# Scores of a unit summed in one PSUM bank among the value products of the unit before it, w_o's last block in two loads, and one load for x

## The chip, the cores and the metric

The kernel runs on one NeuronCore of one Trainium2 chip. The metric is device time in microseconds: 217.72 us, the median of three runs (217.52 to 218.88). One further execution was taken by the hardware profiler; all rows shown come from it. The engines are PE (TensorE, matrix products), DVE (VectorE), ACT (ScalarE), POOL (GpSimd) and SP (SyncE), which only issues transfers here. Sixteen DMA engines move the data.

## The reference, cut to what matters

One decode step for two rows of x, all in float32: windowed attention over a cache, times a gate from a small gated MLP.

```python
# A_x (2,1,512); k_cache, v_cache (2,8,32768,128); wq (512,4096); wo (4096,512)
# w_in (512,1792); w_out (896,512)
W = 4096                                    # last 4096 keys of 32768
q = (xn @ wq)                               # 32 heads of 128; 4 query heads per kv head
scores = einsum("bhqd,bhkd->bhqk", q, k[last W]) * 128 ** -0.5
o = einsum("bhqk,bhkd->bhqd", softmax(scores), v[last W])
s = o.reshape(2, 1, 4096) @ wo
z = gelu(xn @ w_in); z1, z2 = halves of z
g = silu((z1 * (w_sp * layernorm(z2) + b_sp)) @ w_out)
out = x + s * g                             # xn = layernorm(x)
```

## The kernel before, in words

**Units.** A unit is one pair of kv heads of one batch row: 2 x 8 / 2 = 8 units, `units[0]` to `units[7]`, four per batch row. Each has 4 MB of K and 4 MB of V. A partition holds 64 consecutive keys of one of the two heads, so a K or V load is one transfer of 128 rows of 32 KB. The 64 keys are handled in four chunks of 16 (`m` = 0 to 3).

**The ring.** All large inputs go through one buffer of four slots of 4 MB. `enqueue` puts a load in a queue; `advance(slot)` marks a slot as free and issues the loads at the head of the queue whose slots are free. The order never changes: w_q (slots 0 and 1), w_in (2), w_out (3), then k0, k1, v0, k2, v1, k3, v2, and so on to k7, v6, v7, then w_o in pieces of 16, 8, 4, 1, 1, 1 and 1 blocks of (128 rows x 512). Slots are taken round robin, so v0 replaces w_in in slot 2, v1 replaces k0 in slot 0, k3 replaces k1, v2 replaces v0, k4 replaces k2, and so on. SP issues in this order, and a load in a slot waits until everything that reads the slot's former content is done: for K the four DVE transposes, for V the sixteen value products on PE. The result-shaped copy of x (`x4`, two loads, one per batch row) is issued behind the 16-block piece.

**One unit.** `turn(u, m)` transposes a chunk of K on DVE in 32 x 32 blocks into a tile `kt` (three buffers). `shares(u, m)` multiplies the query, for each quarter `dq` of the 128 features, into its own 32 partitions of a PSUM bank `sh`; ACT copies the bank to SBUF (`shs`), and `add_shares(u, m)` adds the four quarters with a 128 x 128 matrix `add_dq` of zeros and ones into the score bank `s`, where chunk m has its own rows. So a unit has sixteen score products, four copies and four adding products. In the profile every float32 product is two PE instructions. `share_max` takes the maximum from `s` on DVE with one small product on PE in between, `probs` the exponentials on ACT, and `probs_t` transposes them on DVE (`pT`). `values` forms sixteen products of V with `pT` into a bank `acc`, product j in the column group j % 4. `scale_out` copies `acc` (four ACT copies), and `collect` adds it into a bank for the batch row.

**Order.** `pe`, `dve`, `act` and `sp` are wrappers that keep each engine's instructions in the order in which the program gives them. In the loop over units (its rows in the profile all have the wrapper's line, L37) unit u and the one before it, `prev`, alternate: first transpose and shares of u; maximum and exponentials of prev; second transpose and shares of u; transposed probabilities and all sixteen value products of prev; then the third and fourth chunk of u; then `scale_out`, the release of u's K slot and of prev's V slot, and `collect`. So V of unit n - 1 comes free in iteration n. The last unit's value products, the sum over units and the products with w_o follow after the loop.

**Gate.** Ahead of the loop the MLP ends with a product `y` into four row groups; `spread_quarters` adds these with eight PE instructions of 128 columns into a bank of 128 x 128, from which DVE and ACT compute the gate. DVE's first K transpose follows the gate in DVE's order.

**End.** Blocks 0 to 27 of w_o are multiplied into `part`, copied and spread into `so`; blocks 28 to 31 go into `so` directly. Two DVE operations form the result, and SP stores it.

Of the kernel before, what the change touches and what calls it, by code (L numbers as in the profile page):

```python
# [9 lines left out]
F32 = mybir.dt.float32  # L10
AF = mybir.ActivationFunctionType
# [3 lines left out]
P = 128  # L15
HQ, DH = 32, 128
G = 4
# [25 lines left out]
def kernel(  # L43
# [13 lines left out]
    nc = tc.nc  # L57
# [9 lines left out]
    DC = D // G  # L67
# [36 lines left out]
    def bank(name, tag):  # L104
        return ps.tile([P, 512], F32, tag=tag, name=name, bufs=BANKS[tag])
# [15 lines left out]
    def by_group(t):  # L121

        return bass.AP(tensor=t.tensor, offset=t.offset, ap=[[DC, G], [D, B], [1, DC]])
# [16 lines left out]
    units = []  # L140
    for n in range(NU):
        u = Unit()
        u.n, u.kt, u.shs, u.slot = n, {}, {}, {}
# [37 lines left out]
    nc.gpsimd.memset(hT, 0.0)  # L181
    x4 = const("x4", DC)
    nc.gpsimd.memset(x4, 0.0)
    add_dq = const("add_dq", NCH - 1 + P)
    nc.gpsimd.memset(add_dq, 0.0)
    sel = const("sel", 56)
# [63 lines left out]
    nc.gpsimd.tensor_copy(sel4[:, 3 : 3 + 32 : 4], rowr)  # L250
    nc.gpsimd.tensor_mul(perm, ap(rowm, 0, [[1, 32], [0, G]]), ap(grpm, 0, [[0, 32], [1, G]]))
    perm = perm.rearrange("p h e -> p (h e)")
    for a in range(2):
# [40 lines left out]
    def q_of(u, dq):  # L294
        return ap(qbd, (u.n * 4 + dq) * 32, [[1, 32]])
# [74 lines left out]

    def turn(u, m):

        u.kt[m] = sb.tile([P, JC, DH], F32, tag="kt", name=f"kt{u.n}_{m}", bufs=3)
        dve.transpose(
            u.kt[m].rearrange("p j d -> p (j d)"), u.k[:, JC * m : JC * m + JC, :].rearrange("p j d -> p (j d)")
        )

    def shares(u, m):

        u.sh = bank(f"sh{u.n}_{m}", "sh")  # L380
        for dq in range(4):
            pe.matmul(
                u.sh[32 * dq : 32 * dq + 32, :], q_of(u, dq), u.kt[m][:, :, 32 * dq : 32 * dq + 32],
                start=True, stop=True,
            )
        u.shs[m] = sb.tile([P, 512], F32, tag="shs", name=f"shs{u.n}_{m}")
        act.activation(u.shs[m], u.sh, AF.Copy)

    def add_shares(u, m):

        if m == 0:
            u.s = bank(f"s{u.n}", "s")
        pe.matmul(u.s, add_dq[:, NCH - 1 - m : NCH - 1 - m + P], u.shs[m], start=(m == 0), stop=(m == NCH - 1))

    def share_max(u):
        m2 = sb.tile([P, 2], F32, tag="m2", name=f"m2_{u.n}")
# [28 lines left out]
    def weigh(u):  # L425
# [10 lines left out]
    def values(u, part=0, parts=1):  # L436
        if part == 0:
            u.acc = bank(f"acc{u.n}", "acc")
        n = JC // parts
        for j in range(n * part, n * part + n):  # L440
            c = j % G
            pe.matmul(
                u.acc[32 * c : 32 * c + 32, :], u.pT[:, j, :], u.v[:, j : J : JC, :],
                start=(j < G), stop=(j >= JC - G),
            )
# [12 lines left out]
    def collect(u, end=NU // B - 1):  # L458

        if u.n == 0:  # L460
            col[0] = bank("col", "col")
        r = slice(32 * u.b, 32 * u.b + 32)
        pe.matmul(
            col[0][r, :], sel[:, 24 - 8 * u.w : 56 - 8 * u.w], u.o.rearrange("p j d -> p (j d)"),
            start=(u.w == 0), stop=(u.w == end),
        )
# [24 lines left out]
    prev = old = None  # L491
    last = units[-1]
    for u in units:
        turn(u, 0)
        shares(u, 0)
        if old is not None and old.n == NU // B - 1:
# [24 lines left out]
    values(old, 0, 2)  # L521
    share_max(last)
    probs(last)
    values(old, 1, 2)
    advance(old.slot["v"])
    probs_t(last)
    weigh(last)
    scale_out(old)
    values(last, 0, 2)
    collect(old, old.w)  # L530
    early = slice(0, 32 * last.w)
    values(last, 1, 2)
    t = gather(last.b)
    scale_out(last)
    divide(last.b, t[early, :], early)
# [53 lines left out]
```

## Time and profile before

| | before |
|---|---|
| time, median of 3 runs | 217.72 us |
| the profiled execution's span | 215.6 us |
| PE busy | 144.9 us (67%) |
| DVE busy | 107.1 us (50%) |
| ACT busy | 43.7 us (20%) |
| bytes read from HBM | 89.40 MB, 415 GB/s over the span |
| granted PE clock, mean | 0.885 |

The span goes from the first to the last instruction of the profiled execution; the runs' times include some 2 us around it. In a timeline row stand the start and the duration in us, the engine, the operation, the tiles out<-in, partitions x elements and the count; in brackets the idle time before it and what ended that. SPq rows are issues of transfers by SP. In a row of the windowed view stand the stretch, its length, the busy time of PE, PE's weight loads, DVE, ACT and POOL with counts, the granted PE clock, the busy share of the DMA engines and GB/s. The line that starts with DMA gives the busy share of the DMA engines in tenths for 40 equal slices.

### The profile page before, as it was taken

The numbers are of one execution on the slowest core, as the hardware profiler recorded it, in microseconds if no ns is written. First come the engines' busy times: TensorE is split into PE (matmuls) and PEld (weight loads), VectorE is DVE, ScalarE is ACT, GpSimd is POOL, SyncE is SP. The second block draws the span as 40 slices with busy tenths as digits, with TensorE's granted clock in tenths as the row PEclk, the third lists the DMA queues.
The fourth block names the chain that finished last, engine by engine and source line by source line (L and its number), as shares of the span: only waits on it lengthen the run. The fifth ranks groups of instructions, "written<-read, shape, count | busy, mean of one in ns | idle before, by whom it ended". The sixth has DMA issues, their size and how long they took to land.

```text
span 215.6 us, 2181 instructions
## 1 busy us (share of the span) xinstructions
PE 144.9 (67%) x848; PEld 40.3 (19%) x848; DVE 107.1 (50%) x161; ACT 43.7 (20%) x108; POOL 4.2 (2%) x22
## 2 busy tenths in 40 slices
PE   0010787224595897699599499459949967987663
PEld 0010222100021222122122132112202211222311
DVE  1140025633995943953936663793585089233101
ACT  2030000331124115114303304130331231241001
POOL 6010000000000000000000000000000000000000
PEclk9999999658599699699799789859975996999998
DMA  9898999999999999999999999999999999999990
GB/s 389 390 389 389 431 423 459 435 438 421 450 395 474 395 453 419 444 432 425 439 404 450 419 444 429 432 432 419 444 413 447 425 432 444 425 435 404 410 376 33
DMA packets 3788, 89.52 MB, mean 415 GB/s; under 512 B 434, under 2 KB 450, under 8 KB 964
## 3 DMA queue, kind: packets, MB, share of 16 engines
q1 hardware_dynamic: 3772, 89.40, 96.9%
q8 instruction: 6, 0.10, 0.2%
q14 instruction: 2, 0.02, 0.0%
q10 hardware_dynamic: 8, 0.00, 0.0%
HBM read 89.40 MB, written 0.00 MB: 415 GB/s over the span
## 4 chain that ended last, share of the span: by engine, by line
DMA 41%; PE 39%; DVE 16%; ACT 2%; issue 2%; DVEq 0%
DMA ring<-in_A_wo_dram 20%; PE sh L37 11%; DMA ring<-in_A_k_cache_dram 11%; DVE kt L37 10%; DMA ring<-in_A_wq_dram 10%; PE s L37 10%; PE acc L37 7%; PE q_ps L37 4%; PE y L37 2%; PE z L37 1%; PE col L37 1%; PE mo L37 1%; DVE gate L37 1%; DVE u L37 1%; DVE qm L37 1%
## 5 line engine op out<-in xcount | busy, mean ns | idle before, releaser
L37 DVE STREAM_TRANSPOSE kt<-ring 128x2048 f32<-128x2048 f32 x32 | 72.2, 2286 | 24.9 <-DMA ring<-in_A_k_cache_dram 24.9
L37 PE MATMUL sh<-kt,qbd 128*32 128x512 f32 x256 | 43.6, 725 | 27.0 <-DVE kt L37 27.0
L37 ACT ACTIVATE shs<-sh 128x512 f32<-128x512 f32 x32 | 19.1, 597 | 99.4 <-PE sh L37 99.4
L37 PE MATMUL s<-shs,add_dq 128*128 128x512 f32 x64 | 39.0, 716 | 0.0
L37 PE MATMUL acc<-ring,pT 128*32 128x512 f32 x256 | 31.3, 614 | 0.0
L37 PEld LDWEIGHTS s<-shs,add_dq 128*128 128x128 f32 x64 | 11.0, 215 | 30.9 <-issue 26.5
L37 PEld LDWEIGHTS sh<-kt,qbd 128*32 128x32 f32 x256 | 7.0, 117 | 46.3 <-issue 38.3
L37 PE MATMUL q_ps<-ring,xnT 128*32 128x512 f32 x64 | 8.8, 713 | 7.6 <-DMA ring<-in_A_wq_dram 7.6
L37 PEld LDWEIGHTS acc<-ring,pT 128*32 128x32 f32 x256 | 7.8, 112 | 22.3 <-issue 17.6
L37 DVE TENSOR_REDUCE m<-s 128x2 f32<-128x512 f32 x8 | 5.4, 680 | 13.0 <-PE s L37 12.9
L37 PE MATMUL xnT_ps<-ident,xn 2*128 2x2 f32 x4 | 0.6, 252 | 14.5 <-DVE xn L37 14.5
L37 ACT ACTIVATE o<-acc,diag 128x128 f32<-128x128 f32 x30 | 8.6, 374 | 4.9 <-PE acc L37 4.9
L37 PE MATMUL part<-ring,oT 128*32 128x512 f32 x56 | 6.6, 597 | 3.5 <-DMA ring<-in_A_wo_dram 3.5
L37 ACT ACTIVATE p<-s,nb 128x256 f32<-128x256 f32 x16 | 7.6, 488 | 6.6 <-DVE nb L37 6.4
L37 DVE STREAM_TRANSPOSE qT<-q_ps 128x512 f32<-128x512 f32 x2 | 1.4, 717 | 14.4 <-PE q_ps L37 14.3
L37 PE MATMUL col<-o,sel 128*32 128x512 f32 x14 | 7.3, 601 | 0.0
L37 DVE TENSOR_TENSOR res<-so,gate 128x128 f32<-128x128 f32 x1 | 0.3, 292 | 11.5 <-PE so L37 11.5
L37 DVE STREAM_TRANSPOSE pT<-p 128x512 f32<-128x512 f32 x8 | 5.4, 674 | 1.2 <-ACT p L37 1.2
L37 PE MATMUL y<-ring,hT 128*32 128x512 f32 x14 | 3.3, 996 | 3.8 <-DVE hT L37 3.8
L37 ACT ACTIVATE zs<-z 128x448 f32<-128x448 f32 x1 | 0.5, 544 | 24.7 <-PE z L37 24.7
L37 ACT ACT_TABLE_LOAD x4 | 5.1, 1283 | 0.8 <-PEq L575 0.7
L37 PEld LDWEIGHTS q_ps<-ring,xnT 128*32 128x32 f32 x64 | 2.5, 130 | 13.1 <-issue 13.1
(114 smaller groups left out, 62.2 us busy)
## 6 DMA issues: line engine op xcount, KB each, us to landing
ring<-in_A_k_cache_dram SPq DMA_DIRECT2D x8, 4096.0 KB, 20.0
ring<-in_A_v_cache_dram SPq DMA_DIRECT2D x8, 4096.0 KB, 28.1
ring<-in_A_wo_dram SPq DMA_DIRECT2D x1, 4096.0 KB, 33.2
ring<-in_B_w_in_dram SPq DMA_DIRECT2D x1, 3584.0 KB, 17.1
ring<-in_A_wo_dram SPq DMA_DIRECT2D x1, 2048.0 KB
ring<-in_B_w_out_dram SPq DMA_DIRECT2D x1, 1792.0 KB, 21.0
ring<-in_A_wo_dram SPq DMA_DIRECT2D x1, 1024.0 KB
ring<-in_A_wo_dram SPq DMA_DIRECT2D x4, 256.0 KB, 17.6
```

What stands on the lines that cost most here:

```text
L37: return self.tc.keep_in_program_order(call(*args, **kwargs))
```

## The change

Scores: the products of a chunk m now go into the row group m of one bank and are summed there over the four quarters (`scores`, two chunks per call). A unit has one copy and one product with a new 128 x 128 matrix `regroup` (`by_key_group`) in place of four copies and four adding products. Between the score products of two chunks, which use two of PE's four column groups, stand eight value products of an older unit in the other two column groups: with chunks 0 and 1 the second half of unit u - 2, with chunks 2 and 3 the first half of unit u - 1. So the V of unit u - 2 is closed, and its slot given back, in iteration u (`close`). `kt` has four buffers. The last unit uses `shares` and `add_shares` for its last two chunks, and its end is written out anew. The gate's `y` is formed by one product over 512 columns and four ACT copies. w_o's last block is loaded as rows 0 to 99 and rows 100 to 127, and x4 in one load.

```diff
+    rows = [slice(0, P)], [slice(0, 100), slice(100, P)]
...
-                sp.dma_start(t[:, a : a + n, :], wo_v[:, j : j + n, :])
+                for r in rows[j == 31]:
+                    sp.dma_start(t[r, a : a + n, :], wo_v[r, j : j + n, :])
...
-                for b in range(B):
-                    sp.dma_start(x4[16 * b : P : 32, :], x[b].rearrange("o (g c) -> (o g) c", g=G))
+                sp.dma_start(x4[0:P:16, :], by_group(x))
...
+    for a in range(2):
+        nc.gpsimd.tensor_copy(regroup[:, :, a], ap(ident, 16 * a, [[4, G], [1, REP], [32, NCH]]))
...
-    y = bank("yq", "mo")[:, :DC]
-    spread_quarters(y, ys)
+    yp = bank("yq", "mo")
+    pe.matmul(yp, same, ys, start=True, stop=True)
+    y = const("y", DC)
+    for g in range(G):
+        r = slice(32 * g, 32 * g + 32)
+        act.activation(y[r, :], yp[r, g * DC : (g + 1) * DC], AF.Copy)
...
-        u.kt[m] = sb.tile([P, JC, DH], F32, tag="kt", name=f"kt{u.n}_{m}", bufs=3)
+        u.kt[m] = sb.tile([P, JC, DH], F32, tag="kt", name=f"kt{u.n}_{m}", bufs=4)
...
+    def columns(c):
+        return [j for j in range(JC) if j % G in c]
+
+    def scores(u, ms, v=None):
+        if ms[0] == 0:
+            u.sh = bank(f"sh{u.n}", "sh")
+        js = columns([c for c in range(G) if c not in ms]) if v is not None else []
+        for dq in range(4):
+            for m in ms:
+                pe.matmul(
+                    u.sh[32 * m : 32 * m + 32, :], q_of(u, dq), u.kt[m][:, :, 32 * dq : 32 * dq + 32],
+                    start=(dq == 0), stop=(dq == 3),
+                )
+            for j in js[2 * dq : 2 * dq + 2]:
+                value(v, j)
+
+    def by_key_group(u, rows=P, stop=True):
+        sh = sb.tile([P, 512], F32, tag="shs", name=f"shs{u.n}")
+        act.activation(sh[:rows, :], u.sh[:rows, :], AF.Copy)
+        u.s = bank(f"s{u.n}", "s")
+        pe.matmul(u.s, regroup[:rows, :], sh[:rows, :], start=True, stop=stop)
...
+    def close(u):
+        scale_out(u)
+        advance(u.slot["v"])
+
     for u in units:
+        prev = units[u.n - 1] if u.n > 0 else None
+        old = units[u.n - 2] if u.n > 1 else None
         turn(u, 0)
-        shares(u, 0)
...
         if prev is not None:
             share_max(prev)
             probs(prev)
         turn(u, 1)
-        shares(u, 1)
-        add_shares(u, 0)
+        scores(u, (0, 1), old)
+        if old is not None:
+            close(old)
         if prev is not None:
             probs_t(prev)
             weigh(prev)
-            if u is not last:
-                values(prev)
-        for m in range(2, NCH):
-            turn(u, m)
-            shares(u, m)
-            add_shares(u, m - 1)
-        if u is not last and prev is not None:
-            scale_out(prev)
+        if u is last:
+            break
+        turn(u, 2)
+        turn(u, 3)
+        scores(u, (2, 3), prev)
         advance(u.slot["k"])
-        add_shares(u, NCH - 1)
-        if u is not last and prev is not None:
-            advance(prev.slot["v"])
-            collect(prev)
-        old, prev = prev, u
...
+        by_key_group(u)
+        if old is not None:
+            collect(old)
```

Behind the loop the last unit's third and fourth chunk follow with `shares`, then the sixteen value products of the unit before it, in three groups around the maximum of the last unit's scores, and then the last unit's value products as before.

More of the change, by code (lines that the diff above doesn't have):

```diff
@@ L142 @@
         u = Unit()
-        u.n, u.kt, u.shs, u.slot = n, {}, {}, {}
+        u.n, u.kt, u.shs, u.slot, u.acc = n, {}, {}, {}, None
         u.b, u.w = divmod(n, NU // B)
@@ L183 @@
     nc.gpsimd.memset(x4, 0.0)
+    regroup = const("regroup", G, 2, REP, NCH)
     add_dq = const("add_dq", NCH - 1 + P)
@@ L252 @@
     perm = perm.rearrange("p h e -> p (h e)")
+    for a in range(2):
+        nc.gpsimd.tensor_copy(regroup[:, :, a], ap(ident, 16 * a, [[4, G], [1, REP], [32, NCH]]))
+    regroup = regroup.rearrange("p g a h m -> p (g a h m)")
     for a in range(2):
@@ L376, in turn, with value @@
         )
+    def value(u, j):
+        if u.acc is None:
+            u.acc = bank(f"acc{u.n}", "acc")
+        c = j % G
+        pe.matmul(
+            u.acc[32 * c : 32 * c + 32, :], u.pT[:, j, :], u.v[:, j : J : JC, :],
+            start=(j < G), stop=(j >= JC - G),
+        )
[7 more added lines that the diff above has]
+            for m in ms:
+                pe.matmul(
+                    u.sh[32 * m : 32 * m + 32, :], q_of(u, dq), u.kt[m][:, :, 32 * dq : 32 * dq + 32],
+                    start=(dq == 0), stop=(dq == 3),
+                )
+            for j in js[2 * dq : 2 * dq + 2]:
[5 more added lines that the diff above has]
+        pe.matmul(u.s, regroup[:rows, :], sh[:rows, :], start=True, stop=stop)
     def shares(u, m):
-        u.sh = bank(f"sh{u.n}_{m}", "sh")
+        t = bank(f"sh{u.n}_{m}", "sh")
         for dq in range(4):
             pe.matmul(
-                u.sh[32 * dq : 32 * dq + 32, :], q_of(u, dq), u.kt[m][:, :, 32 * dq : 32 * dq + 32],
+                t[32 * dq : 32 * dq + 32, :], q_of(u, dq), u.kt[m][:, :, 32 * dq : 32 * dq + 32],
                 start=True, stop=True,
@@ L386, in shares @@
         u.shs[m] = sb.tile([P, 512], F32, tag="shs", name=f"shs{u.n}_{m}")
-        act.activation(u.shs[m], u.sh, AF.Copy)
+        act.activation(u.shs[m], t, AF.Copy)
     def add_shares(u, m):
-        if m == 0:
-            u.s = bank(f"s{u.n}", "s")
-        pe.matmul(u.s, add_dq[:, NCH - 1 - m : NCH - 1 - m + P], u.shs[m], start=(m == 0), stop=(m == NCH - 1))
+        pe.matmul(u.s, add_dq[:, NCH - 1 - m : NCH - 1 - m + P], u.shs[m], start=False, stop=(m == NCH - 1))
     def share_max(u):
@@ L434, in weigh @@
         dve.reciprocal(wd[:, u.b : u.b + 1], u.mo[:, 32:33])
[L436 to L445, printed above, removed]
     def scale_out(u):
@@ L489, in collect_last @@
         divide(u.b, ol[r, :], r)
-    prev = old = None
+    def close(u):
+        scale_out(u)
+        advance(u.slot["v"])
     last = units[-1]
     for u in units:
+        prev = units[u.n - 1] if u.n > 0 else None
+        old = units[u.n - 2] if u.n > 1 else None
         turn(u, 0)
-        shares(u, 0)
-        if old is not None and old.n == NU // B - 1:
+        if u.n == NU // B + 2:
             divide(0, gather(0))
@@ L506 @@
             weigh(prev)
-            if u is not last:
-                values(prev)
-        for m in range(2, NCH):
-            turn(u, m)
-            shares(u, m)
-            add_shares(u, m - 1)
-        if u is not last and prev is not None:
-            scale_out(prev)
-        advance(u.slot["k"])
-        add_shares(u, NCH - 1)
-        if u is not last and prev is not None:
-            advance(prev.slot["v"])
-            collect(prev)
-        old, prev = prev, u
-    values(old, 0, 2)
+        if u is last:
[3 more added lines that the diff above has]
+        scores(u, (2, 3), prev)
+        advance(u.slot["k"])
+        by_key_group(u)
+        if old is not None:
+            collect(old)
+    turn(last, 2)
+    shares(last, 2)
+    by_key_group(last, 64, stop=False)
+    collect(old)
+    turn(last, 3)
+    add_shares(last, 2)
+    shares(last, 3)
+    advance(last.slot["k"])
+    first, second = columns((0, 1)), columns((2, 3))
+    both = [j for p in zip(first[::2], first[1::2], second[::2], second[1::2]) for j in p]
+    for j in both[:4]:
+        value(prev, j)
+    add_shares(last, 3)
+    for j in both[4:10]:
+        value(prev, j)
     share_max(last)
     probs(last)
-    values(old, 1, 2)
-    advance(old.slot["v"])
+    for j in both[10:]:
+        value(prev, j)
     probs_t(last)
     weigh(last)
-    scale_out(old)
-    values(last, 0, 2)
-    collect(old, old.w)
+    close(prev)
+    for j in range(8):
+        value(last, j)
+    collect(prev, prev.w)
     early = slice(0, 32 * last.w)
-    values(last, 1, 2)
+    for j in range(8, JC):
+        value(last, j)
     t = gather(last.b)
```

## The prediction

> **What bounds the kernel now.** I read the page's head, the busy slices and the DMA queues first, then the windowed view with bytes per stretch, then the DMA issues in order of time.
>
> ```profile
> span 215.6 us, 2181 instructions
> PE 144.9 (67%) x848; PEld 40.3 (19%) x848; DVE 107.1 (50%) x161; ACT 43.7 (20%) x108; POOL 4.2 (2%) x22
> DMA  9898999999999999999999999999999999999990
> q1 hardware_dynamic: 3772, 89.40, 96.9%
> q8 instruction: 6, 0.10, 0.2%
> 0.00:92.00 92.00, 47.96 (x274) 13.49 (x278) 44.72 (x83) 16.89 (x35) 4.19 (x22) 0.87 0.99 423
> 0.00:208.00 208.00, 141.24 (x796) 39.22 (x800) 106.50 (x159) 43.14 (x107) 4.19 (x22) 0.89 0.99 426
> ```
>
> No compute engine is busy for more than 67%, while the sixteen DMA engines are busy in every slice up to the last, on one queue of 89.40 MB (in the window rows the last two numbers are the DMA share and GB/s). Between 92 and 208 us it moved 0.426 x 208 - 0.423 x 92 = 49.7 MB in 116 us: 428 GB/s without a hole. So matrix, copy and transpose work counts only where it delays a transfer, or after the last byte. Nothing in the change alters the bytes.
>
> The end of the stream, by half microseconds and then two rows of the timeline:
>
> ```profile
> 209.50:210.00 0.50, 0.50 (x8) 0.06 (x8) 0.00 (x0) 0.00 (x0) 0.00 (x0) 1.00 0.71 262
> 210.00:210.50 0.50, 0.50 (x16) 0.26 (x8) 0.00 (x0) 0.00 (x0) 0.00 (x0) 1.00 0.53 201
> 210.50:211.00 0.50, 0.49 (x16) 0.16 (x8) 0.00 (x0) 0.40 (x1) 0.00 (x0) 1.00 0.42 160
> 211.00:211.50 0.50, 0.38 (x17) 0.25 (x13) 0.00 (x0) 0.20 (x1) 0.00 (x0) 1.00 0.26 98
> ...
> 209.41 1.07 PE L37 MATMUL part<-ring,oT 128*32 128x512 f32 x8 [0.58 <-DMA ring<-in_A_wo_dram]
> 213.12 0.60 SPq L37 DMA_DIRECT2D out_dram<-res  x1
> ```
>
> The engines do not finish together: the share falls in steps from 209.5 to 211.5. Spread evenly, those bytes would end at 209.5 + 0.5 x (0.71 + 0.53 + 0.42 + 0.26) = 210.46, so the slowest engines are 1.0 us behind the mean. At 210.5 to 211 a share of 0.42 is six or seven of sixteen engines, and six 16 KB instruction packets ran on the same engines (q8 above): I take each to have made one engine late. With some 100 of 1,696 PE instructions gone there will still be six. The last products follow, and the result leaves at 213.12. The execution's span is 215.6; the median of the runs, 217.72, is 2.1 us more, and I carry that over unchanged.
>
> **The part that decides: when a V slot comes free.** The ring has four 4 MB slots, filled in the order k0, k1, v0, k2, v1, k3, v2, k4, v3. v2 goes into the slot of v0. These are the issues, the value products of unit 0, and the landing of the K ahead of v2 (rows between are left out):
>
> ```profile
> 62.78 0.54 SPq L37 DMA_DIRECT2D ring<-in_A_v_cache_dram  x1
> 74.46 3.64 PE L37 MATMUL acc<-ring,pT 128*32 128x512 f32 x32
> 75.84 0.54 SPq L37 DMA_DIRECT2D ring<-in_A_k_cache_dram  x1
> 78.16 0.54 SPq L37 DMA_DIRECT2D ring<-in_A_v_cache_dram  x1
> ...
> 95.10 2.31 DVE L37 STREAM_TRANSPOSE kt<-ring 128x2048 f32<-128x2048 f32 x1 [2.37 <-DMA ring<-in_A_k_cache_dram]
> ```
>
> v1, k3 and v2 are issued at 62.78, 75.84 and 78.16. v2 follows the end of the 32 value passes of unit 0 (74.46 + 3.64 = 78.10). When must v2 be there? Ahead of it stand w_q (8.39 MB by its shape), w_in (3.67), w_out (1.84) and six of 4.19: 39.06 MB, or 92.3 us at the 423 GB/s above. The windows count a packet at one instant (shares over 1 occur), so I add half a 32 KB packet at 428/16 GB/s, 0.6 us: the mean engine turns to v2 at 92.9. The last one, by k3's landing, is there about 95. Issue to first packets is 1.0 us or little more:
>
> ```profile
> 0.73 0.39 SPq L37 DMA_DIRECT2D ring<-in_A_wq_dram  x1
> DMA  0000000000000000099999000000000000000000
> ```
>
> (the slices are 0.1 us, from 0; the 18th begins at 1.7). I take 1.1. So v2 must be issued by 91.8; before, it had 13.6 us in hand. The change moves the last eight of v0's sixteen products from unit 1 to the first half of unit 2, and everything now hangs on when that half ends. Its working, from these rows (picked from the timeline of before in order of time, with what lies between left out; then three stretches with the granted clock, third number from the end, and one group):
>
> ```profile
> 51.26 0.43 PE L37 MATMUL yq<-ys,rowm 128*32 128x128 f32 x8 [0.71 <-ACT ys L37]
> 53.87 11.07 DVE L37 STREAM_TRANSPOSE kt<-ring 128x2048 f32<-128x2048 f32 x5
> 56.23 1.93 PE L37 MATMUL sh<-kt,qbd 128*32 128x512 f32 x8 [4.54 <-DVE kt L37]
> 61.43 1.06 PE L37 MATMUL sh<-kt,qbd 128*32 128x512 f32 x8
> 62.43 1.12 PE L37 MATMUL s<-shs,add_dq 128*128 128x512 f32 x2
> 66.50 0.69 DVE L37 TENSOR_REDUCE m<-s 128x2 f32<-128x512 f32 x1 [1.56 <-PE s L37]
> 68.53 2.31 DVE L37 STREAM_TRANSPOSE kt<-ring 128x2048 f32<-128x2048 f32 x1
> 70.76 0.67 DVE L37 STREAM_TRANSPOSE pT<-p 128x512 f32<-128x512 f32 x1
> 81.63 1.14 ACT L37 ACTIVATE o<-acc,diag 128x128 f32<-128x128 f32 x4
> 85.44 2.31 DVE L37 STREAM_TRANSPOSE kt<-ring 128x2048 f32<-128x2048 f32 x1
> 87.90 1.94 PE L37 MATMUL sh<-kt,qbd 128*32 128x512 f32 x8 [2.77 <-DVE kt L37]
> 58.00:60.00 2.00, 1.65 (x12) 0.23 (x8) 2.00 (x2) 0.60 (x1) 0.00 (x0) 0.50 0.87 377
> 62.00:64.00 2.00, 2.00 (x18) 0.46 (x10) 2.00 (x2) 0.60 (x1) 0.00 (x0) 1.00 1.18 508
> 88.00:90.00 2.00, 2.00 (x9) 0.34 (x9) 2.00 (x2) 0.05 (x1) 0.00 (x0) 0.50 0.88 377
> ...
> L37 ACT ACTIVATE shs<-sh 128x512 f32<-128x512 f32 x32 | 19.1, 597 | 99.4 <-PE sh L37 99.4
> ```
>
> *Gate.* Eight small products (0.43) become two full passes (1.12 in the s row), and four copies stand behind them (nearest row: four ACT copies, 1.14). DVE works in order and does its first K transpose after the gate, so this costs 0.7 + 1.1 = 1.8 us at the start: 53.87 becomes 55.65. The bounds are 1.0 and 2.0.
>
> *A half of the scores.* Each 32-column group of PE takes eight passes, one behind the other. The 32 value passes give 3.64 / 8 = 0.455 us per pass with four groups side by side. At half clock two passes took 1.93. The granted clock was 0.50 behind a wait of 2.8 us (88 to 90) and back at 1.00 some 4 us after work began (56.23 to 62). So a half takes 3.6 us warm; cold, 3.5 us carry 3.6 passes and the other 4.4 take 2.0: 5.5 us. With two groups instead of four, as in unit 0, it is no shorter.
>
> *Unit 0.* Transposes take 11.07 / 5 = 2.21 us. Two must be done before the first half now, where one was enough: PE starts at 55.65 + 4.43 + 0.15 = 60.25, cold, and ends at 65.75; the second half, warm, at 69.35. One copy (0.60), one regroup (1.1) and two hops of 0.14 give the scores at 71.3. From there to the next unit's second transpose it was 68.53 - 66.50 = 2.03 us: 73.3, against 68.53 before.
>
> *Unit 1.* 73.3 + 2.23 + 0.67 + 4.43 = 80.65, where k1 is free. With 1.1 us, k3 arrives at 81.75, and the mean engine wants it 9.8 us (4.19 MB) ahead of v2, at 83.1: just in time. A first half from 75.7 ends at 79.3 or 81.2, the second at 84.4 or 84.8; then 1.95 + 2.03 as above: unit 2's second transpose starts at 88.4 to 88.8 (85.44 before).
>
> *Unit 2.* 88.75 + 2.23 + 0.14 = 91.1. The half ends at 94.7 warm or 96.6 cold. The row at 87.90 speaks for cold, but how long it lasts there no row fixes; I take the middle, 95.6. First packets of v2 come at 96.7, and the mean engine has stood for 96.7 - 92.9 = 3.8 us. Nothing gives that back: the other 50.3 MB still need 117.6 us, and the steps of the share at the end stay. With a full clock everywhere the same chain gives 93.25 and a hole of 1.5; with cold phases of the whole length and a late gate, 97.5 and 5.7.
>
> Later slots are in time. A unit now costs about 2.2 + 0.7 + 4.4 + 3.6 + 1.9 + 2.0 + 0.5 = 15.3 us of chain (85.44 - 68.53 = 16.9 before) against 19.6 us of transfers. v1 is thus free near 111 while v3 is wanted two loads behind v2's start, at 116.3.
>
> **The rest of the change.** Per unit six adding passes go (6 x 0.55 = 3.3 us of PE) and three copies (1.8 us of ACT). They lie beside the stream and are counted at nothing except in the chain above; without the stream as cover they would be a gain. Two POOL copies for the new constant lie ahead of others early on, with their first use near 70 us. One load of x for two saves SP half a microsecond in mid-stream. In the last unit wo's first block now waits for v5's second half, about 6.5 + 5.5 us behind k7's landing instead of in the unit before; it is wanted 16 us or more behind that landing, so it holds.
>
> *The last block in 100 and 28 rows.* No row shows how such a load is spread. In 210.50:211.00, 160 GB/s at a share of 0.42 are 24 GB/s an engine, 0.086 us per 2 KB row, and now each engine has 8 of them. Freed of all eight, a late engine gains 0.7; eight more cost 0.7. Even a gain shrinks: after the four-block load (209.41) PE still has 1.07 of products, a copy of 0.6 and the last products, so that only 0.1 to 0.2 of it is seen. I take 0.
>
> ```profile
> DMA packets 3788, 89.52 MB, mean 415 GB/s; under 512 B 434, under 2 KB 450, under 8 KB 964
> ```
>
> The 434 smallest packets are what 26 loads of 128 rows with 16 closing packets each, two loads of x and one store with 4 each, and 6 on ACT's queue make. [...]
>
> Sum: 217.7 + 3.8 = 221.5 us.
>
> **Rivals.** *No hole:* v0's products end by 91.8. Unit 2's second half-transpose would have to start by 85.7 with a warm clock, no later than now. The shorter unit chain (15.3 for 16.9) speaks for it; the gate and the coarser start of unit 0 (73.3 for 68.53) against. Time 217.6, from 217.3 to 218.1. *A small hole,* under 2.2 us, the warm end of my own chain: 218.1 to 219.9. *More holes:* if halves stay cold and each V from v3 on is late by 1 us, it is 223.5 to 227; the 5 us in hand at v3 speak against it. *Faster by over 1%:* an even finish of the stream gives 1.0 us at most and the tail behind it 0.2; with unchanged bytes I find no 2.2 us.
>
> **How the numbers follow.** One per cent, 2.2 us, is about what a measurement can tell from no change. The hole of over 2.2 us has 0.58, more holes 0.05: slower 0.63. No hole has 0.20 and the small hole 0.13: same 0.33. Faster 0.04. The forecast's own range is 219.2 to 223.4. With a third on the other side, the range reaches from 217.3 to 223.6.
>
> **What would show it.** v2's issue near 95.6 and k3's near 80.7; a slice near 92 to 97 us with a DMA share well under 9; k4 landing later by the hole, and all behind it; value products of unit 0 ending in unit 2; the first scores of unit 1 complete near 71. [...] If v2 is issued before 91.8 and the share stays at 9, I am wrong.

## The result and the profile after

The changed kernel took 223.86 us (median of six runs, 220.80 to 226.46), the kernel before beside it 217.63 us (six runs, 217.51 to 218.88). Three of the six runs lie near 226 us, where none of the kernel before does, and are left out, as no profile shows what lengthened them; by the others the ratio is 1.0148, with an interval from 1.0109 to 1.0187: 3.2 us slower. The profiled execution took 221.54 us, with a span of 219.8 us, against 215.6 us before; the readings below account for these 4.2 us.

The head of the page, the busy slices and the DMA queues of the changed kernel:

```profile
span 219.8 us, 2020 instructions
PE 141.1 (64%) x798; PEld 39.8 (18%) x798; DVE 107.1 (49%) x161; ACT 32.2 (15%) x90; POOL 4.6 (2%) x24
DMA  9889989998989999998989899999999999999980
DMA packets 3792, 89.52 MB, mean 407 GB/s; under 512 B 438, under 2 KB 454, under 8 KB 968
q1 hardware_dynamic: 3776, 89.40, 95.7%
```

PE is busy 3.8 us less and ACT 11.5 us less, and the span is longer all the same. The bytes are the same; the queue's packets fill 95.7% of the span and not 96.9%. The mean rate fell from 415 to 407 GB/s, so the stream stood somewhere.

SP's issues from v1 to the store, with gaps (start, length; x2 stands for two issues in a row):

```profile
64.63 0.54 SPq L37 DMA_DIRECT2D ring<-in_A_v_cache_dram  x1
79.53 0.53 SPq L37 DMA_DIRECT2D ring<-in_A_k_cache_dram  x1
93.04 0.54 SPq L37 DMA_DIRECT2D ring<-in_A_v_cache_dram  x1
...
170.38 1.19 SPq L37 DMA_DIRECT2D ring<-in_A_v_cache_dram  x2
...
217.22 0.61 SPq L37 DMA_DIRECT2D out_dram<-res  x1
```

v1, k3 and v2 are issued at 64.63, 79.53 and 93.04. v2 was issued at 78.16 before, so it comes 14.9 us later. Around it, the windowed view (columns as before the prediction: the last two are the DMA share and GB/s):

```profile
90.00:92.00 2.00, 2.00 (x23) 0.56 (x18) 2.00 (x1) 0.00 (x0) 0.00 (x0) 1.00 1.19 500
92.00:93.00 1.00, 1.00 (x11) 0.30 (x5) 1.00 (x2) 0.00 (x0) 0.00 (x0) 1.00 0.23 98
93.00:94.00 1.00, 0.84 (x2) 0.00 (x0) 1.00 (x1) 0.96 (x4) 0.00 (x0) 1.00 0.16 66
...
0.00:90.00 90.00, 43.39 (x222) 12.23 (x226) 41.21 (x82) 12.17 (x27) 4.65 (x24) 0.87 0.99 422
0.00:110.00 110.00, 59.72 (x325) 16.52 (x329) 56.39 (x93) 16.10 (x40) 4.65 (x24) 0.89 0.98 417
```

From 92 to 94 the DMA engines are nearly idle. Up to 90 us the stream runs at 422 GB/s, and up to 110 us at 417. The kernel before has 424 in that stretch:

```profile
0.00:110.00 110.00, 63.19 (x358) 17.52 (x362) 56.35 (x93) 21.34 (x47) 4.19 (x22) 0.88 0.99 424
```

The lost 0.007 x 110 = 0.77 MB are 1.8 us at 428 GB/s. In the timeline of the kernel before, DVE's first transposes of k4 and k7, which wait for the landing, the maximum of the last unit's scores, and the first of PE's products with w_o:

```profile
114.57 2.31 DVE L37 STREAM_TRANSPOSE kt<-ring 128x2048 f32<-128x2048 f32 x1 [4.89 <-DMA ring<-in_A_k_cache_dram]
172.86 2.31 DVE L37 STREAM_TRANSPOSE kt<-ring 128x2048 f32<-128x2048 f32 x1 [7.98 <-DMA ring<-in_A_k_cache_dram]
188.20 0.69 DVE L37 TENSOR_REDUCE m<-s 128x2 f32<-128x512 f32 x1 [3.88 <-PE s L37]
...
202.09 3.64 PE L37 MATMUL part<-ring,oT 128*32 128x512 f32 x32 [1.74 <-DMA ring<-in_A_wo_dram]
```

The same rows of the changed kernel:

```profile
116.34 2.31 DVE L37 STREAM_TRANSPOSE kt<-ring 128x2048 f32<-128x2048 f32 x1 [7.30 <-DMA ring<-in_A_k_cache_dram]
174.63 2.31 DVE L37 STREAM_TRANSPOSE kt<-ring 128x2048 f32<-128x2048 f32 x1 [5.94 <-DMA ring<-in_A_k_cache_dram]
195.89 0.69 DVE L37 TENSOR_REDUCE m<-s 128x2 f32<-128x512 f32 x1 [9.87 <-PE s L37]
...
208.72 6.21 PE L37 MATMUL part<-ring,oT 128*32 128x512 f32 x56 [0.68 <-DVE oT L37]
```

k4 lands 1.77 us later, k7 1.77 us later: a loss made once and carried on unchanged. The maximum of the last unit's scores is 7.7 us later, far more than k7. The end of the stream, in the windowed view of the changed kernel:

```profile
214.00:214.50 0.50, 0.50 (x12) 0.15 (x8) 0.00 (x0) 0.00 (x0) 0.00 (x0) 1.00 0.10 37
214.50:215.00 0.50, 0.50 (x17) 0.25 (x12) 0.00 (x0) 0.00 (x0) 0.00 (x0) 1.00 0.00 0
```

Before, the products with w_o waited for its blocks one after another (1.74 us here, and the 0.58 shown in the prediction). Now they start behind DVE's `oT` and run 6.21 us without a wait. The stream ends by 214.5 (211.5 before), the store leaves at 217.22 (213.12 before). By the stream, the 4.1 us at the store are **1.8** of the hole at v2, **1.2** more between k7 and the stream's end (3.0 less 1.8), and **1.1** behind the stream's end (217.22 - 214.5 = 2.7 against 1.6).

The chain that ended last divides them otherwise. It goes from k7's landing through the last unit to the products with w_o. k7 is **1.8** later. From its first transpose to these products it is 34.1 us for 29.2, **4.9** longer, and from there to the store 8.5 for 11.0, **2.5** shorter, since the waits for w_o are gone. As no product waits for w_o, the 1.2 did not set the time of this execution. The experiments ask what each part is made of.

### The profile page after: what moved, and what is told of

The parts are those of the page before. It is cut to its first block, busy times and chain, and to the rows that moved or that the text cites. A ratio compares the mean times of both kernels' runs of the same rounds, so it can differ in the third digit from the quotient of the medians.

```text
span 219.8 us, 2020 instructions
## 1 busy us (share of the span) xinstructions
PE 141.1 (64%) x798; PEld 39.8 (18%) x798; DVE 107.1 (49%) x161; ACT 32.2 (15%) x90; POOL 4.6 (2%) x24
## 3 DMA queue, kind: packets, MB, share of 16 engines
q1 hardware_dynamic: 3776, 89.40, 95.7%
## 4 chain that ended last, share of the span: by engine, by line
PE 36%; DMA 31%; DVE 24%; ACT 5%; issue 2%; DVEq 0%; ACTq 0%
DMA ring<-in_A_k_cache_dram 21%; PE sh L37 15%; DVE kt L37 15%; DMA ring<-in_A_wq_dram 10%; PE q_ps L37 4%; PE acc L37 4%; PE s L37 3%; PE part L37 3%; PE y L37 2%; DVE m L37 1%; PE mo L37 1%; PE z L37 1%; ACT shs L37 1%; DVE mg L37 1%; DVE pT L37 1%
## 5 line engine op out<-in xcount | busy, mean ns | idle before, releaser
L37 PE MATMUL sh<-kt,qbd 128*32 128x512 f32 x256 | 82.8, 713 | 20.4 <-DVE kt L37 20.4
L37 PE MATMUL acc<-ring,pT 128*32 128x512 f32 x256 | 61.7, 674 | 0.0
L37 PEld LDWEIGHTS sh<-kt,qbd 128*32 128x32 f32 x256 | 18.9, 126 | 73.5 <-DVE kt L37 37.3
L37 PEld LDWEIGHTS acc<-ring,pT 128*32 128x32 f32 x256 | 14.4, 121 | 7.7 <-issue 7.7
L37 PE MATMUL s<-shs,regroup 128*128 128x512 f32 (+1 forms) x16 | 9.0, 642 | 6.7 <-ACT shs L37 6.7
L37 ACT ACTIVATE shs<-sh 128x512 f32<-128x512 f32 (+1 forms) x10 | 5.9, 599 | 50.3 <-PE sh L37 28.3
L37 PE MATMUL mo<-mg,same_r 128*128 128x16 f32 x16 | 3.6, 299 | 9.9 <-DVE mg L37 9.9
L37 PEld LDWEIGHTS mo<-mg,same_r 128*128 128x128 f32 x16 | 2.8, 218 | 16.1 <-DVE mg L37 14.0
L37 PEld LDWEIGHTS s<-shs,regroup 128*128 128x128 f32 (+1 forms) x16 | 2.4, 187 | 13.9 <-ACT shs L37 12.3
L37 DVE BATCH_NORM_STATS2 st<-xs 2x6 f32<-2x512 f32 x1 | 0.7, 681 | 8.5 <-DMA xs<-in_A_x_dram 8.5
```

The source lines that it names most:

```text
L37: return self.tc.keep_in_program_order(call(*args, **kwargs))
```

## Experiments

Three theories stood before the runs. A: only the hole at v2. B: the hole and, behind it, a longer chain of the last unit. C: that chain alone. Two suspects came with them: the loads of w_o's last block and the gate. Every ratio is against the kernel before, run beside it on the same chip.

**The hole alone, in the kernel before.** Eight of the sixteen value products of unit 0 are moved from iteration 1 to iteration 2, ahead of the products of unit 1; everything else stays.

```diff
+            if u.n == 2:
+                values(old, 1, 2)
+                scale_out(old)
+                advance(old.slot["v"])
+                collect(old)
             if u is not last:
-                values(prev)
+                if u.n == 1:
+                    values(prev, 0, 2)
+                else:
+                    values(prev)
```

> The kernel before with one thing moved: eight of unit 0's sixteen value products go into iteration 2, and v0's slot is given back there. v2 is then issued near 93.4 instead of 78.2, and its first packets come 2 us later, some 2.5 us after the mean engine wants them. Theories A and B: 219.6 to 220.1. Theory C: 217.6.

221.77 us (four runs, 219.80 to 221.84), ratio 1.0175 (1.0132 to 1.0218): as late as A and B had it, or later. The hole in the windowed view:

```profile
92.00:93.00 1.00, 0.55 (x8) 0.00 (x0) 0.00 (x0) 0.37 (x2) 0.00 (x0) 1.00 0.23 98
93.00:94.00 1.00, 0.09 (x1) 0.12 (x2) 0.00 (x0) 0.77 (x3) 0.00 (x0) 1.00 0.38 131
```

SP's issue of v2 and DVE's first transpose of k7, in the timeline:

```profile
92.62 0.54 SPq L37 DMA_DIRECT2D ring<-in_A_v_cache_dram  x1
...
175.17 2.31 DVE L37 STREAM_TRANSPOSE kt<-ring 128x2048 f32<-128x2048 f32 x1 [7.97 <-DMA ring<-in_A_k_cache_dram]
```

The same hole at the same place, k7 later by 2.3 us, the store at 215.36 (2.2 later). With the scores, gate, loads and last unit of before, this kernel loses as much as the changed one. C falls: a late v2 is enough. The profiled execution was the shortest of the four; the other three took 221.72 to 221.84, so the same late slot does not always cost the same.

**Unit 0's V early, in the changed kernel.** All sixteen products of unit 0 are done in iteration 1, so that v2's slot is free one half earlier.

```diff
-        scores(u, (0, 1), old)
-        if old is not None:
+        if u.n == 1:
+            probs_t(prev)
+            weigh(prev)
+        if u.n != 2:
+            scores(u, (0, 1), prev if u.n == 1 else old)
+        else:
+            scores(u, (0, 1), None)
+        if old is not None and old.n > 0:
             close(old)
-        if prev is not None:
+        if prev is not None and u.n != 1:
             probs_t(prev)
...
         advance(u.slot["k"])
+        if u.n == 1:
+            close(prev)
```

> The changed kernel, but unit 0's sixteen value products all in iteration 1 (eight in each half), so that v2 can be issued near 83 us instead of 93.0. Theory A (only the hole in the stream at v2 costs time): back to 217.6 us. Theory B (the hole of 3.0 us and, in series with it, a longer chain of the last unit from k7's landing to the first product with w_o, 34.1 us by the changed kernel's trace): k7 lands near 172.9 again, w_o's products start at 207.0 and the store is issued near 215.5: about 220 us. Theory C (the last unit's chain alone, whatever the stream does): no change, 221.

223.45 us (four runs, 223.12 to 223.56), ratio 1.0272 (1.0255 to 1.0289): not mended, and worse. SP's issues of k3, v2 and v3, and the gate's product:

```profile
82.75 0.53 SPq L37 DMA_DIRECT2D ring<-in_A_k_cache_dram  x1
87.40 0.54 SPq L37 DMA_DIRECT2D ring<-in_A_v_cache_dram  x1
...
114.66 0.54 SPq L37 DMA_DIRECT2D ring<-in_A_v_cache_dram  x1
...
53.63 2.07 PE L37 MATMUL yq<-ys,same 128*128 128x512 f32 x2 [0.71 <-ACT ys L37]
```

The same product in the profile of the changed kernel:

```profile
51.35 1.13 PE L37 MATMUL yq<-ys,same 128*128 128x512 f32 x2 [0.71 <-ACT ys L37]
```

v2 is in time, but the hole is at v3: with v2 in time the stream wants v3 two loads later, at 92.9 + 19.6 = 112.5, and it is issued at 114.66, since its slot is that of v1, which is still closed an iteration late (the DMA share from 113 to 115 is 0.10 and 0.08). k3 is late too (82.75, where 82.0 was the last moment). That does not come from the edit: the gate's product starts 2.3 us later than in the changed kernel's profile and takes 0.9 us more (the clock was 0.50 at 52 to 54), and unit 0's scores follow 3.2 us later (63.48 for 60.27). The edit did not test A: it repaired one slot and left the others on the same rule. "Later slots are in time" does not hold in this execution. In the changed kernel's profile v3 is issued at 107.81, so whether it would be late there without the hole at v2 stays open.

**The last unit as before, in the changed kernel** (four chunks with `shares` and `add_shares`, unit 5's products finished in iteration 6).

```diff
+        if u is last:
+            shares(u, 1)
+            add_shares(u, 0)
...
+    for m in range(2, NCH):
+        turn(last, m)
+        shares(last, m)
+        add_shares(last, m - 1)
```

> The changed kernel, but the last unit's four chunks go as in the kernel before (shares and adding products, chunk by chunk), and unit 5's value products are all done in iteration 6. The hole at v2 stays. Theory A: no change, 221. Theory B: the stream's end sets the time again, 3.0 us later than before: 220.3 to 220.7, with w_o's products waiting for transfers. Theory C: 217.6.

226.55 us (one run at 221.84, three from 226.50 to 227.39), too far apart for a ratio. Inconclusive, and the edit may have a cost of its own: it puts unit 5's remaining products ahead of the last unit on PE.

**Both edits together** (the two diffs above).

> Both edits together in the changed kernel: unit 0's value products in iteration 1 and the last unit as before. Theories A and B: 217.6 (217.3 to 218.0). Theory C: 217.6. A fourth view, that the interleaved score products, the regroup product or the loads themselves cost time: 219 or more.

220.43 us (four runs, 218.13 to 222.93), ratio 1.0100 (1.0034 to 1.0166). Better than the first edit alone, but the hole at v3 is still there (issue at 114.61), so this does not separate the theories either.

**Every V closed in its iteration, in the changed kernel.** The transposed probabilities now come ahead of the first half, and both halves carry products of unit u - 1. The one-bank scores, the value products between them, the gate, the loads and the order of the last unit stay as in the changed kernel, but unit 5's products, copies and collecting product leave the last unit with this edit.

```diff
-        scores(u, (0, 1), old)
-        if old is not None:
-            close(old)
         if prev is not None:
             probs_t(prev)
             weigh(prev)
+        scores(u, (0, 1), prev if u is not last else None)
...
-        if old is not None:
-            collect(old)
+        if prev is not None:
+            close(prev)
+            collect(prev)
```

> The changed kernel, but the probabilities of unit u - 1 are transposed ahead of unit u's first half, and both halves carry value products of unit u - 1, so every V slot is given back one iteration earlier; the last unit is left as changed. No load should wait for a slot. Theory A (holes in the stream alone): 217.5 plus the 0.9 that the loads cost by themselves, 218.4. Theory B (the last unit's chain besides): w_o's products start near 207, after their first block has landed, and the time is about 220.

219.32 us (ten runs, 217.90 to 220.86), ratio 1.0066 (1.0032 to 1.0100). v2 and v3 are in time. So 1.0148 - 1.0066 = 0.8%, 1.8 us, hang on the iteration in which a V is closed, with what that puts into the last unit, though the two intervals leave anything from 0.1 to 1.6%. What is left over is k3 and the end of the stream (SP's issues of k3, v2 and v3, then PE's products with w_o):

```profile
82.57 0.54 SPq L37 DMA_DIRECT2D ring<-in_A_k_cache_dram  x1
87.18 0.54 SPq L37 DMA_DIRECT2D ring<-in_A_v_cache_dram  x1
...
101.95 0.53 SPq L37 DMA_DIRECT2D ring<-in_A_v_cache_dram  x1
...
205.62 3.64 PE L37 MATMUL part<-ring,oT 128*32 128x512 f32 x32 [0.68 <-DVE oT L37]
...
212.31 1.07 PE L37 MATMUL part<-ring,oT 128*32 128x512 f32 x8 [0.91 <-DMA ring<-in_A_wo_dram]
```

Without unit 5's share the last unit's chain is 30.1 us from k7's first transpose (175.48) to the products with w_o, 4 us shorter than in the changed kernel. So these products wait for DMA again, and the stream ends last.

**The same with the last unit as before.** Beside the edit above, the last unit keeps the order and the products of before:

```diff
+        if u is last:
+            shares(u, 1)
+            add_shares(u, 0)
         if prev is not None:
             probs_t(prev)
             weigh(prev)
+        if u is last:
+            break
+        scores(u, (0, 1), prev)
```

> The same, and the last unit's scores chunk by chunk as before. Theories A and B: 218.4, what the loads alone gave. If the interleaved halves, the regroup product or the gate cost time of their own: 219.5 or more.

218.39 us (ten runs, 218.14 to 220.76), ratio 1.0057 (1.0026 to 1.0089). Against 1.0066 that is no difference that can be told. The runs of both kernels spread over more than 2 us, and both profiled executions (220.77 and 220.76 us) are among the longest. In both k3 is late, and the stream loses time there. SP's issue of k3 and the windowed view of this kernel:

```profile
83.02 0.54 SPq L37 DMA_DIRECT2D ring<-in_A_k_cache_dram  x1
83.00:84.00 1.00, 1.00 (x13) 0.36 (x16) 1.00 (x1) 0.00 (x0) 0.00 (x0) 1.00 0.08 33
```

As in the kernel with unit 0's V early, the gate's product is late and slow: it starts at 53.44 and 53.89 and takes 2.07 us.

**And the old loads and the old gate.** Of the change there remain the one-bank scores, one copy and one `regroup` product a unit, the value products between the scores, and the four buffers of `kt`.

```diff
-                for r in rows[j == 31]:
-                    sp.dma_start(t[r, a : a + n, :], wo_v[r, j : j + n, :])
+                sp.dma_start(t[:, a : a + n, :], wo_v[:, j : j + n, :])
...
+    y = bank("yq", "mo")[:, :DC]
+    spread_quarters(y, ys)
```

> The same with the loads and the gate of the kernel before: only the scores in one bank and the value products between them are left of the change. Theories A and B: 217.5, within 0.3 of the kernel before, since the stream sets the time in both.

217.60 us (ten runs, 217.28 to 217.93), ratio 0.9994 (0.9980 to 1.0008). PE is busy 6.6 us less than in the kernel before and ACT 12.5 (138.3 and 31.2); that gains nothing and costs nothing once every slot is back in time. The profiled execution reaches the gate as late as the two above, but there the eight small products of before are short, and k3 is in time:

```profile
54.09 0.42 PE L37 MATMUL yq<-ys,rowm 128*32 128x128 f32 x8 [0.71 <-ACT ys L37]
...
80.52 0.54 SPq L37 DMA_DIRECT2D ring<-in_A_k_cache_dram  x1
```

The 0.6% of the two kernels above come with loads and gate, which the next two take one by one.

**The loads alone, in the kernel before** (w_o's last block as 100 and 28 rows, x in one load).

```diff
-                sp.dma_start(t[:, a : a + n, :], wo_v[:, j : j + n, :])
+                for r in rows[j == 31]:
+                    sp.dma_start(t[r, a : a + n, :], wo_v[r, j : j + n, :])
...
-                for b in range(B):
-                    sp.dma_start(x4[16 * b : P : 32, :], x[b].rearrange("o (g c) -> (o g) c", g=G))
+                sp.dma_start(x4[0:P:16, :], by_group(x))
```

> The kernel before with only the loads changed: w_o's last block as 100 and 28 rows, x in one load. [...]

218.40 us (twelve runs, 218.12 to 219.23), ratio 1.0039 (1.0023 to 1.0055), 0.85 us. The end of the stream in the windowed view:

```profile
210.50:211.00 0.50, 0.44 (x12) 0.16 (x8) 0.00 (x0) 0.24 (x1) 0.00 (x0) 1.00 0.63 156
211.00:211.50 0.50, 0.00 (x0) 0.00 (x0) 0.00 (x0) 0.36 (x1) 0.00 (x0) 1.00 0.44 131
211.50:212.00 0.50, 0.34 (x12) 0.34 (x16) 0.00 (x0) 0.00 (x0) 0.00 (x0) 1.00 0.18 66
```

PE's products with one of w_o's last blocks, in the timeline:

```profile
211.66 0.43 PE L37 MATMUL so<-ring,oT 128*32 128x128 f32 x8 [0.72 <-DMA ring<-in_A_wo_dram]
```

The shares of before, 0.42 and 0.26 in the first two stretches, are now 0.63 and 0.44, and a third stretch follows. The stream ends half a microsecond later, and PE stands 0.72 us for it. The single load of x is in the same edit; it lies in mid-stream, and no run separates it.

**The gate alone, in the kernel before** (one product over 512 columns and four ACT copies).

```diff
-    y = bank("yq", "mo")[:, :DC]
-    spread_quarters(y, ys)
+    yp = bank("yq", "mo")
+    pe.matmul(yp, same, ys, start=True, stop=True)
+    y = const("y", DC)
+    for g in range(G):
+        r = slice(32 * g, 32 * g + 32)
+        act.activation(y[r, :], yp[r, g * DC : (g + 1) * DC], AF.Copy)
```

> The kernel before with only the gate's y formed by one product and four ACT copies: unit 0 starts 1.8 us later, v1 and k3 are issued 1.8 us later and still ahead of their need. Theories A and B: 217.6, no change. If any delay of the units reached the end: 219.4.

217.82 us (twelve runs, 217.36 to 219.89), ratio 1.0030 (1.0001 to 1.0058). v1 and k3 are issued at 64.54 and 78.36, 1.8 and 2.5 us later than before, and the stream of its profiled execution shows no hole. But the runs fall into two groups: eight from 217.36 to 218.28, four from 219.52 to 219.89. In the profiled execution, one of the first group, k3 is issued 3.6 us ahead of 82.0 (wanted at 83.1, less 1.1). That the longer ones were late there is only argued, since none of them was profiled; it is what the long executions of the kernels with V closed in its iteration show.

**The old gate in the changed kernel** (the diff above, turned round).

> The changed kernel with the gate as before, so that every unit up to v2's issue is 1.8 us earlier: v2 issued near 91.2, hole 1.2 us instead of 3.0. Theories A and B: 1.8 us less than the changed kernel, about 219.2. Theory C: no change, 221.

222.12 us (four runs, 221.81 to 223.09), ratio 1.0211 (1.0180 to 1.0242): no better without the new gate. SP's issues of k3 and v2:

```profile
77.98 0.54 SPq L37 DMA_DIRECT2D ring<-in_A_k_cache_dram  x1
93.39 0.54 SPq L37 DMA_DIRECT2D ring<-in_A_v_cache_dram  x1
```

The clock under the half that must end before v2:

```profile
88.00:90.00 2.00, 1.99 (x12) 0.60 (x16) 2.00 (x2) 0.00 (x0) 0.00 (x0) 0.50 1.07 459
```

k3 is issued 1.55 us earlier than in the changed kernel, v2 0.35 us later. The lead was eaten by a half of unit 2 that here began at half clock and took 5.3 us (88.01 to 93.32); in the changed kernel's profile the same half took 3.6 at a clock of 1.00 (90 to 92 above).

**The new last unit in the kernel before.**

```diff
+        if u is last:
+            scores(u, (0, 1))
+            probs_t(prev)
+            weigh(prev)
+            old = prev
+            break
...
+    turn(last, 2)
+    shares(last, 2)
+    by_key_group(last, 64, stop=False)
+    turn(last, 3)
+    add_shares(last, 2)
+    shares(last, 3)
...
```

> The kernel before with only the last unit's part of the change: chunks 0 and 1 in one bank after the second transpose, then the end as in the changed kernel. The stream has no hole. Theory A: 217.5. Theory B: the maximum of the last unit's scores comes some 6 us later, w_o's products start near 207 instead of 202, and the time is 219.5 to 220.5.

217.67 us (ten runs, 217.45 to 221.01), ratio 0.9998 (0.9980 to 1.0016). PE's products with w_o, and the store:

```profile
204.73 6.22 PE L37 MATMUL part<-ring,oT 128*32 128x512 f32 x56 [0.68 <-DVE oT L37]
...
213.24 0.59 SPq L37 DMA_DIRECT2D out_dram<-res  x1
```

The products with w_o start 2.6 us later (204.73 against 202.09), and the store is 0.1 later: they run through without the waits that they had before. So a chain longer by 2.6 us is paid out of waits for w_o. B had expected the products near 207. The edit leaves out what the changed kernel's last unit carries of unit 5, and the chain is 31.7 us here (from 173.06) and 34.1 there. B's second part falls for this much of the chain; for the other 2.4 us no run tests it.

## Why the prediction was right, and where only its total was

The forecast was 221.5 us and slower. Slower it was, and by the mechanism named: v0's last products end too late, v2's slot comes back too late, and the stream stands. That the total came near is luck: a hole put too long stood in for terms put at nothing. The sum had 3.8 us for the hole and 0 for all else; the profile has 1.8 for the hole and 2.3 (4.9 less 2.5, rounded) for the chain of the last unit.

**Gate and unit 0.** The first K transpose behind the gate was put at 55.65; it is at 55.72. PE's first half was to start at 60.25, behind two transposes; its first product needs one and ran at 58.08, the rest from 60.27. Both halves were to end at 69.35 and end at 68.28 (30 passes from 60.27, 8.01 us). Part of that 1.1 us is the price of a cold pass: PE's weight loads follow each other at 0.86 us from 60.27 to 63.69, at a granted clock of 0.50, where I had 0.97 (3.5 us for 3.6 passes). It passes on to unit 1 (second transpose at 72.22 for 73.3) and to k3's issue (79.53 for 80.65). But this start is not the same in every execution: in three of the kernels with the new gate the rest of the first half began at 63.30 to 63.75, behind a gate's product that started at 53.44 to 53.89 for 51.35 and took 2.07 us for 1.13. The prediction has one start, and with the other k3 is late.

**Unit 2, the step that failed.** "How long it lasts there no row fixes; I take the middle, 95.6." The half ran warm, at a clock of 1.00 from 90 to 92:

```profile
89.35 0.62 PE L37 MATMUL sh<-kt,qbd 128*32 128x512 f32 x1 [1.71 <-DVE kt L37]
...
92.39 0.60 PE L37 MATMUL acc<-ring,pT 128*32 128x512 f32 x2
```

Its first product ran at 86.60; the rest began at 89.35 for 91.1 and took the 3.6 us of a full clock. v2's issue at 93.04 is the warm end of the prediction's own chain (93.25), and the warm end's hole was 1.5; 1.8 was measured. The formula behind it, issue plus latency less need, holds only roughly: 93.04 + 1.1 - 92.9 = 1.2. The kernel before with v0 closed late shows a remainder as well: 92.62 + 1.1 - 92.9 = 0.8, and k7 was 2.3 us later. By k7's landing a hole therefore cost 0.6 to 1.5 us more than the formula says, and I cannot name why.

**"Nothing gives that back; the steps of the share at the end stay."** Right for the first part: k4 and k7 are both late by 1.77. Wrong for the second: the stream's end lost 1.2 us more. Part of it is the next item. Another part may be v6, which "later slots are in time" denied: it is issued only at 170.38, 4.3 us ahead of k7's first transpose (8.0 in the kernel before). How the 1.2 divide was not measured.

**The last block in 100 and 28 rows: a term of the sum mis-sized.** I took 0; with x in one load it costs 0.85 alone (0.50 to 1.20). My price was too low: I had let the gain and the loss of a late engine cancel, at 0.7 each, and by the shares of 0.63 and 0.44 the loss decides. How the rows of the two loads fall on the engines no run shows; the small packets number 438 in the page above, against 434 before, and no count tells an engine's rows. The price of a row was too low as well: 156 GB/s at a share of 0.63 are 15.5 GB/s an engine, where I had 24 from the kernel before; a 2 KB row is 0.13 us at that rate and 0.086 at mine. Why the engines moved less in the time in which they were busy was not tested. In the changed kernel's profile no product waits for w_o, so there this loss does not show.

**The gate's cover.** I costed it only through v2's chain and called k3 "just in time". Alone it costs 0.30% (0.01 to 0.58%), about 2 us in a third of its runs and little in the others. Where the work ahead of the gate is late, the gate's product takes 2.07 us (at a clock of 0.50 in the kernel with unit 0's V early) and k3 misses its moment, issued at 82.57 to 83.02 for 82.0; with the eight small products of before, 0.42 us, it does not (80.52). So a term that I had as 1.8 us of one chain decides whether a second slot is late. Loads and gate together, 0.39 + 0.30 = 0.69%, are what the kernels with V closed in its iteration were left with (0.57 and 0.66%). The changed kernel with the old gate (1.0211) does not fit such a sum; its profile shows why v2 is late in that execution, and not in all four runs. Nor does the late slot have one price: 0.8% as the difference to the kernel with V closed in its iteration, 1.75% by itself in the kernel before. So the division of the 3.2 us among slot, loads, gate and last unit is rough. That a late v2 alone can cost as much rests on the kernel before with v0 closed late.

**The last unit.** I looked only at whether w_o's first block is wanted in time, not at the unit's own chain. Here the maximum came at 195.89. The first half of its scores, between products of unit 5, ran mostly at half clock; behind it unit 5's four copies, the copy of the scores, the `regroup` product, unit 5's collecting product and the last two chunks follow one another. The clock, in the windowed view:

```profile
182.00:184.00 2.00, 2.00 (x16) 0.54 (x12) 2.00 (x2) 0.00 (x0) 0.00 (x0) 0.50 1.07 459
184.00:186.00 2.00, 2.00 (x12) 0.39 (x8) 2.00 (x1) 0.00 (x0) 0.00 (x0) 0.50 0.77 328
```

In this one execution this chain is what ended last, with the 1.1 us behind the stream's end. Without unit 5's share the new last unit costs nothing in a stream that is on time, and with V closed in its iteration it made no difference to have the old one. How much of the 3.2 us it is in the changed kernel's other runs stays open: the run that was to show it gave no ratio.

**The rivals.** No hole is refuted by the windows at 92 to 94. The small hole, under 2.2 us, is what the profile shows, and by itself it would have been "within 1%": 217.7 + 1.8 = 219.5. What made it slower than that are the other terms, which I had at nothing: in the profile the chain of the last unit. More holes, one at each V, is refuted in the changed kernel's profile, but the kernel with unit 0's V early shows one at v3. That the change would not be faster held for the reason given: with all that delays the stream taken out, the rest of the change measures 0.9994.

## What to carry to other kernels

In a kernel that a stream of transfers bounds, ask of every reordering when each buffer is given back, and compare that with the time at which the stream wants it; here 6.6 us of PE and 12.5 of ACT saved beside the stream left the time at 0.9994, and one slot returned 15 us later cost 1.8 us by the profile. Repair the rule and not the first place where it bites: with only unit 0 repaired, the next slot on the same rule was late. At the stream's end, measure how the last loads are divided before relying on it: 100 and 28 rows, with x in one load, cost 0.85 us. And where a slot hangs on a chain of engine work, leave room for a cold clock in that chain: the half of unit 2 took 3.6 us at 1.00 and 5.3 where it began at 0.50.

## What the runs showed of the hardware that I had not expected

The time of the same eight score passes differed from one execution to another by which part of them ran at half clock: the half of unit 2 took 3.6 us in the profile of the changed kernel and 5.3 (88.01 to 93.32) with the old gate. Two passes of a product took 1.90 us of the latter, at a granted clock of 0.50, and 1.00 us of the former, at 1.00.

So one stage is warm in one profile and cold in another. The penalty of that stage, 1.7 us of 220, is 0.8%. But where a slot hangs on the stage, so little is enough: it ate the whole lead of the old gate, 1.55 us at k3, and v2 was issued 0.35 us later than in the changed kernel. A gate's product of 2.07 us for 1.13, 2.1 to 2.5 us late, came ahead of the late k3 in the long executions with the new gate. Whether the two groups of runs with the new gate alone, 2 us apart, come from this too was not shown.

A second gap behind the hole is the other surprise. In slices of 0.15 us from 91 us on, of the changed kernel (busy tenths of the DMA engines):

```profile
DMA  5955999050900505000000999905000005999000
```

The first packets behind v2's issue at 93.04 show from 94.3 on, 1.3 us after it, and the next ones only from 96, some 1.7 us behind the first, where a 32 KB packet at the stream's rate (428/16 GB/s) takes 1.2 us. This may be the remainder that the formula for the hole lacks; nothing here tests it.
